# Window attention feeding a rational-activation MLP on one core: the sink rows of V in one transfer per batch, V in two pieces per head, another program order

## The chip, the cores and the metric

The kernel runs on one NeuronCore of a Trainium2 chip. The metric is device time in microseconds (us) of one execution. TensorE (PE) does the matrix products, VectorE (DVE) and ScalarE (ACT) the elementwise work, GpSimd (POOL) issues the loads that change float32 into bfloat16, and SyncE (SP) issues plain transfers and DMA transposes. Each engine runs its own instructions strictly in the order in which the program lists them, and waits on semaphores for the others.

## The reference

Four batches, eight heads, 768 tokens, head width 64. A token attends to itself, to the 127 tokens before it, and to the first four tokens of its sequence (the sink rows). The attention output, as 3072 rows of 512, goes through a two-layer network with a rational function between its layers.

```python
scores = q @ k.T / sqrt(64)
keep = (pos_k < 4) | ((pos_q - pos_k >= 0) & (pos_q - pos_k < 128))
a = softmax(where(keep, scores, -1e9)); x = (a @ v)     # per batch and head
x = x.transpose(0, 2, 1, 3).reshape(3072, 512)
h = x @ w_in                                            # 512 -> 2048
P = a0 + a1*h + a2*h**2 + a3*h**3
Q = 1 + |b0|*|h| + |b1|*h**2
out = (P / (Q + 1e-6)) @ w_out                          # 2048 -> 512
```

## The kernel before, in words

**Steps.** The 3072 tokens are cut into 12 steps of 256; three steps make a batch. For step s, four pieces `scores(s, 0..3)` (L561, L569, and L551 for the sink keys) fill a PSUM bank with masked scores, `exps(s, i)` (L581, ACT) turns each into weights, two pieces `attend(s, G)` (L622) multiply them with V, `norm(s, G)` (L630, L631, DVE) divides by the sums, and `turn_x` with `placed_x` transposes the result into `xblk`. Then four pieces `gemm1(s, j)` (L681, 16 matmuls each) make h, `copy_in` (L688, ACT) takes it out of PSUM, DVE and ACT compute the rational function (L695 to L735, with the division done as exp of minus ln on ACT), and `gemm2(s, ...)` (L742) multiplies with w_out. Step 0 and step 11 do the rational function in four parts, the others in one.

**Order.** Every piece of work is registered by `piece(...)`, with the engine that issues it. `ORDER` is a list of 728 numbers that was worked out beforehand: it names the registered pieces one by one, and a negative number stands for that many warming matmuls on a scratch tile (`spin`, L529). The table `BANK` names the PSUM buffer of a piece and `ENGINE` whether a copy runs on DVE or ACT. So the list fixes the sequence on every engine and in every queue. Data dependences, buffers that must come free, and a limited number of DMA semaphores (a later transfer that reuses one waits until the earlier one has landed) add the waits.

**The first loads.** The first 256 keys and 384 queries of batch 0 come in float32 through the queues of SP and ACT, half of the heads each (`load_k0`, L298; `load_q0`, L308), are cast (`cast_k0`, `cast_q0`, L482 on ACT, L484 on DVE), turned on TensorE with the identity (L466) and placed. Later keys and queries come through POOL (`load_kc` L333, `load_qc` L341, from step 4 on `load_k` L350 and `load_q` L320, which SP turns by DMA transposes). V comes through POOL per head (`load_v`, L357), in batch 0 as 256 tokens and then 512, in the batches 1 to 3 as all 768 in one transfer. The weights come through POOL in four transfers each (`load_w_in` L363, `load_w_out` L369).

**The sink rows of V.** `load_v_sink(b)` (L375) loads the four first rows of V of all heads, 32 rows of 64 numbers, into `stage_s`, and it does so four times, once into each group of 32 partitions: 16 transfers of 8 KB for four batches, those of batch 0 in ACT's queue, the rest in SP's. `spread_v_sink(b)` (L379, DVE) multiplies them with an indicator into `v_sink`.

**Queues before**, read off the list. SP: `load_q0(0)`, `load_k0(0)`, 12 sink-row transfers, then transposes. ACT: `load_b`, `load_q0(1)`, 4 sink-row transfers, `load_k0(1)`, `cast_q0(0)`, `load_a`, `cast_k0(1)`, then copies and exps. TensorE: 67 warming matmuls, `turn_q0` twice, 20 warming matmuls, `turn_k0` twice, `scores(0, 1)`, and so on. `ones_v(1)` (L279), which writes the ones column of the second V buffer, is the 55th piece of DVE; four of the eight V loads of batch 1 stand behind it.

Of the kernel before, what the change touches and what calls it, by code (L numbers as in the profile page):

```python
# [60 lines left out]
def kernel(  # L61
# [65 lines left out]
    BANK = {('attend', 0, 0): 'ps_o',  # L127
             ('attend', 0, 1): 'ps_h',
             ('attend', 1, 1): 'ps_h',
             ('attend', 2, 0): 'ps_o',  # L130
             ('attend', 3, 0): 'ps_h',
             ('attend', 4, 0): 'ps_h',
             ('attend', 4, 1): 'ps_h',
             ('attend', 5, 0): 'ps_h',
             ('attend', 6, 0): 'ps_o',
             ('attend', 6, 1): 'ps_o',
             ('attend', 7, 1): 'ps_h',
             ('attend', 8, 1): 'ps_o',
             ('attend', 9, 0): 'ps_o',
             ('attend', 9, 1): 'ps_o',  # L140
             ('attend', 10, 0): 'ps_h',
             ('attend', 11, 0): 'ps_o',
             ('gemm1', 0, 0): 'ps_o',
             ('gemm1', 0, 2): 'ps_m',
             ('gemm1', 0, 3): 'ps_h',
             ('gemm1', 1, 0): 'ps_m',
             ('gemm1', 1, 1): 'ps_h',
             ('gemm1', 1, 2): 'ps_o',
             ('gemm1', 1, 3): 'ps_h',
             ('gemm1', 2, 0): 'ps_o',  # L150
             ('gemm1', 2, 1): 'ps_m',
             ('gemm1', 2, 2): 'ps_o',
             ('gemm1', 2, 3): 'ps_h',
             ('gemm1', 3, 0): 'ps_m',
             ('gemm1', 3, 1): 'ps_m',
             ('gemm1', 3, 2): 'ps_m',
             ('gemm1', 4, 0): 'ps_o',
             ('gemm1', 4, 2): 'ps_m',
             ('gemm1', 4, 3): 'ps_h',
             ('gemm1', 5, 0): 'ps_m',  # L160
             ('gemm1', 5, 3): 'ps_h',
             ('gemm1', 6, 0): 'ps_o',
             ('gemm1', 6, 2): 'ps_m',
# [12 lines left out]
             ('gemm1', 11, 1): 'ps_h',
             ('gemm1', 11, 2): 'ps_m',
             ('gemm1', 11, 3): 'ps_h',
             ('gemm2', 1, 0, 0): 'ps_o',
             ('gemm2', 2, 0, 0): 'ps_m',  # L180
             ('gemm2', 5, 0, 0): 'ps_m',
             ('gemm2', 7, 0, 0): 'ps_o',
# [5 lines left out]
             ('scores', 1, 1): 'ps_m',
             ('scores', 2, 0): 'ps_m',
             ('scores', 2, 2): 'ps_m',  # L190
             ('scores', 2, 3): 'ps_o',
             ('scores', 4, 1): 'ps_m',
# [4 lines left out]
             ('scores', 6, 1): 'ps_o',
             ('scores', 6, 2): 'ps_o',
             ('scores', 6, 3): 'ps_m',
             ('scores', 7, 0): 'ps_h',  # L200
             ('scores', 7, 3): 'ps_o',
             ('scores', 8, 2): 'ps_o',
             ('scores', 9, 2): 'ps_o',
# [1 line left out]
             ('scores', 10, 2): 'ps_m',
             ('scores', 10, 3): 'ps_h',
             ('scores', 11, 1): 'ps_m',
             ('turn_k0', 1): 'ps_h',
             ('turn_kc', 1, None): 'ps_h',
# [3 lines left out]
             ('turn_qc', 3, 0): 'ps_o',
             ('turn_x', 0, 0): 'ps_o',
             ('turn_x', 1, 0): 'ps_h',
             ('turn_x', 2, 0): 'ps_o',
# [935 lines left out]
```

## Time and profile before

| | us |
|---|---|
| three timed runs: median (lowest, highest) | 257.23 (256.55, 257.94) |
| the profiled execution's own time | 258.26 |
| its span, first to last instruction | 256.5 |
| first `exps` on ACT starts | 20.25 |
| `gemm1(0, 3)` starts | 54.12 |
| TensorE busy in the span | 230.7 |
| DVE busy, ACT busy | 211.8, 210.6 |

The profile is of one execution. Times in it count from the first instruction of the span. The page's second part cuts the span into 40 slices of 6.4 us and gives a digit of busy share per slice, the granted clock of TensorE and the rate of the DMAs. The chain of waits follows the work that ended last back to its releasers.

### The profile page before, as it was taken

To read this page: it belongs to the slowest core of one execution; us is meant where nothing else is said; L and a number is where in the kernel's file an instruction comes from. 1 tells how busy PE (TensorE), PEld (TensorE's weight loads), DVE (VectorE), ACT (ScalarE), POOL (GpSimd) and SP (SyncE) were. 2 spreads that over 40 slices of the span, in tenths; PEclk is the share of its full clock that TensorE was granted. 3 is DMA by queue.
4 is the path that set the end of the run, shared out by engine and by line. 5 is a ranking of instruction groups with operands and counts; after the bars stand their busy time and mean duration, and the time that the engine had idled before them with its cause. 6 is when DMAs were issued, how large, how long until landed. Compare 5 with 4: busy or idle time off the path is not lost.

```text
span 256.5 us, 7754 instructions
## 1 busy us (share of the span) xinstructions
PE 230.7 (90%) x3475; PEld 156.2 (61%) x3475; DVE 211.8 (83%) x243; ACT 210.6 (82%) x171; POOL 73.2 (29%) x100
## 2 busy tenths in 40 slices
PE   7548479689999987999999999999999999999993
PEld 7447257568867563764855757747875657754431
DVE  2164405999989998989977999999799999999991
ACT  2117426999999898889899999999999998998980
POOL 8964571009430721349302492000000000000000
PEclk9875957999999999999999999999999999999999
DMA  5999999249999999959999599784130303001222
GB/s 140 158 183 201 125 181 91 19 64 65 160 197 149 98 178 106 109 63 121 104 170 107 63 189 118 88 166 132 28 111 3 103 1 105 0 0 55 112 82 82
DMA packets 98753, 27.12 MB, mean 106 GB/s; under 512 B 89504, under 2 KB 95648, under 8 KB 98720
## 3 DMA queue, kind: packets, MB, share of 16 engines
q0 software_dynamic: 67920, 12.98, 85.1%
q1 hardware_dynamic: 29152, 12.69, 27.4%
q10 hardware_dynamic: 1648, 0.95, 1.4%
q8 instruction: 27, 0.44, 0.8%
q14 instruction: 6, 0.05, 0.1%
HBM read 27.40 MB, written 6.29 MB: 131 GB/s over the span
## 4 chain that ended last, share of the span: by engine, by line
PE 70%; ACT 13%; DVE 6%; DMA 6%; issue 3%; SPq 0%; ACTq 0%; DVEq 0%
PE ps_o L681 11%; PE ps_m L681 10%; PE ps_h L742 10%; PE ps_m L742 9%; PE ps_h L681 8%; PE ps_o L742 8%; DMA stage_s<-in_v_dram 3%; DMA stage_a<-in_k_dram 3%; ACT hb L688 3%; ACT den L730 3%; ACT e L581 2%; PE ps_s L561 2%; ACT lnq L725 2%; PE ps_m L622 2%; DVE x_n L631 1%
## 5 line engine op out<-in xcount | busy, mean ns | idle before, releaser
L681 PEld LDWEIGHTS <-w_in_sb 128*128 128x128 bf16 x768 | 74.8, 100 | 15.0 <-issue 1.7
L742 PEld LDWEIGHTS <-g 128*128 128x128 bf16 x384 | 35.7, 98 | 43.9 <-DVE g L735 2.5
L725 ACT ACTIVATE lnq<-den,one_eps,qsc 128x4096 f32<-128x4096 bf16 (+1 forms) x18 | 47.9, 2665 | 0.1
L730 ACT ACTIVATE den<-lnq 128x4096 bf16<-128x4096 f32 (+1 forms) x18 | 44.7, 2481 | 0.1
L357 POOL DMA_DIRECT2D v<-in_v_dram x40 | 31.7, 803 | 21.7 <-DVE den L702 18.4
L681 PE MATMUL ps_o<-xblk,w_in_sb 128*128 128x256 bf16 x304 | 37.4, 278 | 0.2 <-DMA v<-in_v_dram 0.2
L742 PE MATMUL ps_h<-w_out_sb,g 128*128 128x512 bf16 x160 | 37.1, 380 | 0.2 <-DVE g L735 0.2
L681 PE MATMUL ps_m<-xblk,w_in_sb 128*128 128x256 bf16 x272 | 34.2, 281 | 0.9 <-ACT e L581 0.9
L742 PE MATMUL ps_m<-w_out_sb,g 128*128 128x512 bf16 x128 | 30.1, 380 | 0.2 <-DVE g L735 0.2
L735 DVE TENSOR_TENSOR g<-num,den 128x4096 bf16<-128x4096 bf16 (+1 forms) x18 | 28.1, 1573 | 0.7 <-ACT den L730 0.6
L719 DVE TENSOR_TENSOR sq<-sq,hb 128x4096 bf16<-128x4096 bf16 (+1 forms) x18 | 28.3, 1574 | 0.2
L706 DVE TENSOR_TENSOR den<-den,sq 128x4096 bf16<-128x4096 bf16 (+1 forms) x18 | 28.3, 1571 | 0.2
L722 DVE TENSOR_TENSOR num<-num,sq 128x4096 bf16<-128x4096 bf16 (+1 forms) x18 | 28.2, 1572 | 0.0
L581 ACT ACTIVATE e<-ps_s 128x768 bf16<-128x768 f32 (+1 forms) x24 | 21.0, 875 | 4.5 <-PE ps_s L569 4.5
L742 PE MATMUL ps_o<-w_out_sb,g 128*128 128x512 bf16 x96 | 22.4, 379 | 1.9 <-issue 1.9
L350 POOL DMA_DIRECT2D k_bf<-in_k_dram x16 | 15.0, 942 | 31.2 <-DMA kT<-k_bf 29.0
L681 PE MATMUL ps_h<-xblk,w_in_sb 128*128 128x256 bf16 x192 | 23.0, 273 | 0.3 <-ACT hb L688 0.3
L688 ACT ACTIVATE hb<-ps_m 128x1024 bf16<-128x1024 f32 x17 | 17.4, 1023 | 6.3 <-PE ps_m L681 6.2
L688 ACT ACTIVATE hb<-ps_o 128x1024 bf16<-128x1024 f32 x19 | 19.5, 1026 | 2.6 <-PE ps_o L681 2.4
L702 DVE TENSOR_SCALAR den<-hb 128x2048 uint32<-128x2048 uint32 (+1 forms) x18 | 15.9, 882 | 6.9 <-ACT hb L688 6.9
L561 PEld LDWEIGHTS <-kT 64*64 64x64 bf16 x384 | 11.8, 112 | 14.0 <-issue 10.4
L695 ACT ACTIVATE sq<-hb 128x1024 bf16<-128x1024 bf16 (+1 forms) x15 | 20.0, 1350 | 0.0
(115 smaller groups left out, 308.9 us busy)
## 6 DMA issues: line engine op xcount, KB each, us to landing
out_dram<-o_t SPq DMA_DIRECT2D x11, 512.0 KB
v<-in_v_dram POOLq DMA_DIRECT2D x24, 96.0 KB, 7.2
w_in_sb<-in_moe_w_in_dram POOLq DMA_DIRECT2D x4, 512.0 KB, 9.1
k_bf<-in_k_dram POOLq DMA_DIRECT2D x16, 128.0 KB, 8.2
w_out_sb<-in_moe_w_out_dram POOLq DMA_DIRECT2D x4, 512.0 KB, 11.8
q_bf<-in_q_dram POOLq DMA_DIRECT2D x15, 128.0 KB, 8.4
k_raw<-in_k_dram POOLq DMA_DIRECT2D x3, 256.0 KB, 5.8
v<-in_v_dram POOLq DMA_DIRECT2D x8, 64.0 KB, 11.0
```

What stands on the lines that cost most here:

```text
L357: nc.gpsimd.dma_start(out=v_fix[b % 2][half(r), g * NHF:(g + steps) * NHF, hl, 0:D], in_=v[b, h, g * TS:(g + steps) * TS, :].rearrange("(j ...
L581: nc.scalar.activation(out=data, in_=ps[:, :, c0:512], func=AF.Exp, scale=inv_sqrt_d)
L681: nc.tensor.matmul(ps[:, n, :], lhsT=w_in_all[:, c, fc * P:(fc + 1) * P], rhs=xblk[m][:, c, :], start=(c == 0), stop=(c == NDMC - 1))
L688: nc.scalar.activation(out=hb[m][:, j * GW:(j + 1) * GW], in_=ps_h.pop((m, j)).rearrange("p n c -> p (n c)"), func=AF.Copy)
L695: nc.scalar.activation(out=sq[m][:, c], in_=hb[m][:, c], func=AF.Square)
L706: nc.vector.tensor_tensor(out=den[m][:, c], in0=den[m][:, c], in1=sq[m][:, c], op=ALU.add)
L719: nc.vector.tensor_tensor(out=sq[m][:, c], in0=sq[m][:, c], in1=hb[m][:, c], op=ALU.mult)
L722: nc.vector.tensor_tensor(out=num[m][:, c], in0=num[m][:, c], in1=sq[m][:, c], op=ALU.add)
L725: nc.scalar.activation(out=lnq_fix[:, c], in_=den[m][:, c], func=AF.Ln, scale=qsc, bias=one_eps)
L730: nc.scalar.activation(out=den[m][:, c], in_=lnq_fix[:, c], func=AF.Exp, scale=-1.0)
L735: nc.vector.tensor_tensor(out=g_of[m][:, c], in0=num[m][:, c], in1=den[m][:, c], op=ALU.mult)
L742: nc.tensor.matmul(ps_out[m][:, tt, :], lhsT=g_of[m][:, co:co + P], rhs=w_out_all[:, fc, :], start=(fc == 0), stop=(fc == NFFC - 1))
```

## The change

- `load_v_sink(b)` becomes one transfer per batch, into 32 partitions. A matmul with the constant `spread` (four 32 x 32 identities side by side) copies the 32 rows into all four groups of partitions in PSUM, once for batch 0 and once for the batches 1 to 3; `spread_v_sink` reads them there. New: a cast of the rows, the making of `spread`, two matmuls (`turn_vs`).
- V of every batch comes as 256 tokens and then 512 per head: 24 transfers of 768 tokens become 24 of 256 and 24 of 512.
- `ones_v` writes both V buffers in one piece, which stands first on DVE.
- `load_a` and `load_b` get a later place than the first loads.
- New `ORDER`, `BANK` and `ENGINE`.

```diff
+    SR = P // NPB
     ENGINE = {('cast_k0', 1): 'ACT',
+               ('cast_q0', 0): 'DVE',
                ('cast_q0', 1): 'DVE',
-               ('place_k0', 0): 'ACT',
-               ('place_k0', 1): 'DVE',
-               ('place_kc', 1, None): 'ACT',
+               ('place_k0', 1): 'ACT',
+               ('place_kc', 2, None): 'ACT',
                ('place_kc', 3, None): 'ACT',
-               ('place_qc', 1, None): 'ACT',
+               ('place_qc', 0, 0): 'ACT',
+               ('place_qc', 0, 1): 'ACT',
                ('place_qc', 2, None): 'ACT',
-               ('place_qc', 3, 0): 'ACT',
+               ('place_qc', 3, 1): 'ACT',
...
-    def ones_v(n):
-        nc.vector.memset(v_fix[n].rearrange("p j h c -> p (j h) c")[:, :, D:D + 1], 1.0)
+    def ones_v():
+        for t_ in v_fix:
+            nc.vector.memset(t_.rearrange("p j h c -> p (j h) c")[:, :, D:D + 1], 1.0)
...
-    stage_s = const_pool.tile([P, B, D], FP32, name="stage_s")
+    stage_s = const_pool.tile([SR, B, D], FP32, name="stage_s")
+    sink_rows = const_pool.tile([SR, B, D], BF16, name="sink_rows")
+    spread = const_pool.tile([SR, NPB, SR], BF16, name="spread")
...
     def load_v_sink(b):
-        for i in range(NPB):
-            (nc.sync if b else nc.scalar).dma_start(out=stage_s[i * SR:(i + 1) * SR, b, :],
-                                                    in_=v[b, :, 0:NS, :])
-
-    def spread_v_sink(b):
-        nc.vector.tensor_tensor(
-            out=v_sink[:, b, :, 0:D], in0=stage_s[:, b, :].unsqueeze(1).to_broadcast([P, H, D]),
-            in1=ind.unsqueeze(2).to_broadcast([P, H, D]), op=ALU.mult)
+        (nc.sync if b else nc.scalar).dma_start(out=stage_s[:, b, :], in_=v[b, :, 0:NS, :])
+
+    def spread_tile():
+        nc.vector.tensor_copy(out=spread, in_=ident[0:SR, 0:SR].unsqueeze(1).to_broadcast(
+            [SR, NPB, SR]))
...
+    def cast_v_sink(part):
+        bs = sink_batches(part)
+        nc.vector.tensor_copy(out=sink_rows[:, bs, :], in_=stage_s[:, bs, :])
...
+    def turn_v_sink(part, bank):
+        bs = sink_batches(part)
+        ps_v[part] = full_bank(bank)[:, 0:(bs.stop - bs.start) * D].rearrange(
+            "p (b d) -> p b d", d=D)
+        nc.tensor.matmul(ps_v[part], lhsT=spread.rearrange("p i c -> p (i c)"),
+                         rhs=sink_rows[:, bs, :], start=True, stop=True)
+
+    def spread_v_sink(part):
+        bs = sink_batches(part)
+        for b in range(bs.start, bs.stop):
+            nc.vector.tensor_tensor(
+                out=v_sink[:, b, :, 0:D],
+                in0=ps_v[part][:, b - bs.start, :].unsqueeze(1).to_broadcast([P, H, D]),
+                in1=ind.unsqueeze(2).to_broadcast([P, H, D]), op=ALU.mult)
...
-        if s == 1 or g == 0:
-            n = 2 if s == 1 else 3
-            old = [("ones_v", 1)] if b == 1 else [("attended", GPB * (b - 2) + g_)
+        if g < 2:
+            n = g + 1
+            old = [("ones_v",)] if b == 1 else [("attended", GPB * (b - 2) + g_)
                                                  for g_ in range(GPB)] if b else []
             for h in range(H):
                 piece(("load_v", s, h), "POOL", 0.75, r_ + 1.0,
...
     def v_loads(s):
         b, g = divmod(s, GPB)
-        return [("load_v", GPB * b + (1 if b == 0 and g else 0), h) for h in range(H)]
+        return [("load_v", GPB * b + min(g, 1), h) for h in range(H)]
```

**The new sequence**, read off the new list up to the point where step 0's first product is complete:

```
SP    load_vs(3) load_vs(1) load_k0(0) load_vs(2) load_q0(0), then transposes
ACT   load_q0(1) load_vs(0) load_k0(1) load_b cast_k0(1) load_a place_k0(1) place_qc(0,1) place_qc(0,0)
      exps(0,3) (0,2) babs exps(0,0) (1,0) place_kc(2) place_qc(2) exps(1,3) (1,1) (0,1) (1,2) (2,2) (2,0)
      placed_x(0,1) copy_in(0,1) (0,2) exps(2,3) place_qc(3,1) ln ln exps(2,1) copy_in(0,0) exp sqa
      place_kc(3) copy_in(0,3)
POOL  constants, then kc1, kc2, qc1, qc2, the identity and the 16 V loads of batch 0, mixed, then w_in 1, w_in 2, qc3, w_in 0, kc3, w_in 3, 2 V loads of batch 1, k and q
      of step 4, 4 V loads, w_out 3, V, V(6,3) of batch 2, V, w_out 1, w_out 0, w_out 2, ...
PE    turn_k0(1) turn_q0(1) turn_k0(0) 19 warming matmuls turn_q0(0) turn_kc(1) scores(0,3) (0,2) turn_qc(1)
      scores(0,0) (1,0) turn_vs(0) turn_kc(2) turn_vs(1) turn_qc(2) scores(1,3) (0,1) (1,1) attend(0,1)
      scores(2,0) (1,2) (2,2) attend(0,0) attend(1,1) turn_x(0,0) (0,1) attend(1,0) gemm1(0,1) (0,2)
      turn_x(1,0) scores(2,3) turn_qc(3) twice attend(2,0) scores(2,1) gemm1(0,0) turn_kc(3) attend(2,1)
      turn_x(1,1) gemm1(0,3)
```

In the list before, `gemm1(0, 3)` also stands behind the other three pieces of `gemm1(0)`, all scores of the steps 0 to 2 and the attends of the steps 0 and 1; of what differs, `scores(3, 3)` stands ahead of it there, and `attend(2, 1)` in the new list. ACT's pieces up to `copy_in(0, 3)` are in the new list the exps of the steps 0 to 2, three copies out of PSUM, two ln, one exp, one square. In the list before they are the same and one exps of step 3, one ln and one exp of step 0 more.

## Rows read from the trace of the kernel before

**Rows 1.** The page, busy time per engine, and rates per slice of 6.4 us.
```profile
PE 230.7 (90%) x3475; PEld 156.2 (61%) x3475; DVE 211.8 (83%) x243; ACT 210.6 (82%) x171; POOL 73.2 (29%) x100
...
GB/s 140 158 183 201 125 181 91 19 64 65 160 197 149 98 178 106 109 63 121 104 170 107 63 189 118 88 166 132 28 111 3 103 1 105 0 0 55 112 82 82
```

**Rows 2.** Busy time of each engine in four stretches, granted clock, DMA.
```profile
core 0: us, PE busy (x) PEld busy (x) DVE busy (x) ACT busy (x) POOL busy (x), PEclk, DMA share, GB/s
0.00:20.25 20.25, 12.16 (x127) 11.01 (x129) 6.20 (x20) 3.35 (x5) 16.76 (x35) 0.86 1.30 163
20.25:54.12 33.87, 24.44 (x626) 18.64 (x626) 18.94 (x43) 22.48 (x28) 11.20 (x15) 0.78 1.47 115
54.12:252.24 198.12, 194.11 (x2728) 126.58 (x2726) 186.02 (x180) 184.12 (x139) 45.28 (x51) 1.00 1.10 98
252.24:256.50 4.26, 0.00 (x0) 0.00 (x0) 0.69 (x1) 0.60 (x1) 0.00 (x0) 1.00 0.32 123
```

**Rows 3.** The chain that ended last: start us, length us, what.
```profile
0.80 0.46 SPq L308
...
1.85 7.32 DMA stage_s<-in_v_dram
...
9.92 7.11 DMA stage_a<-in_k_dram
17.05 0.64 ACT early L482
...
29.37 3.68 issue
...
36.20 3.57 PE ps_m L681 x16
...
54.12 1.76 PE ps_h L681 x16
```

**Rows 4.** Timeline of the first 21 us: start, length, engine, line, [idle before].
```profile
1.22 7.14 PE L529 MATMUL ps_s<-warm 128*128 128x128 bf16 x67 [1.22 <-DVE warm L859]
...
1.87 8.01 ACTq L375 DMA_DIRECT2D stage_s<-in_v_dram  x4
...
9.06 0.70 DVE L484 CAST early<-stage_b 128x768 bf16<-128x768 f32 x1 [3.67 <-DMA stage_b<-in_q_dram]
...
12.13 0.85 PE L466 MATMUL ps_m<-ident,early 128*128 128x128 bf16 x6
...
14.56 0.95 DVE L484 COPY qT<-ps_m 128x768 bf16<-128x768 bf16 x1
...
20.25 0.81 ACT L581 ACTIVATE e<-ps_o 128x768 bf16<-128x768 f32 x1 [0.85 <-PE ps_o L569]
```

**Rows 5.** The line that loads w_in, its fourth transfer alone.
```profile
L363 POOL DMA_DIRECT2D w_in_sb<-in_moe_w_in_dram x1: 752/752/752, 29.9 to 29.9; - x1
...
DMA to landing us min/median/max: 8.2/8.2/8.2
```

**Rows 6.** Who waited for whom: total us, times, longest.
```profile
POOL v L357 <- DVE den L702: 18.4, 1, 18.4
...
ACT hb L688 <- PE ps_m L681: 6.2, 6, 3.7
...
ACT e L581 <- PE ps_s L569: 4.5, 2, 4.3
```

**Rows 7.** DMA issues: count, KB each, median us to landing.
```profile
v<-in_v_dram POOLq DMA_DIRECT2D x24, 96.0 KB, 7.2
...
v<-in_v_dram POOLq DMA_DIRECT2D x8, 32.0 KB, 6.0
```

**Rows 8.** Busy time and clock in three stretches of the start.
```profile
12.00:15.00 3.00, 2.82 (x30) 2.65 (x27) 1.05 (x2) 0.00 (x0) 3.00 (x6) 0.60 1.51 183
18.00:21.00 3.00, 2.31 (x40) 1.77 (x37) 0.69 (x1) 1.35 (x3) 2.94 (x5) 0.50 1.34 198
...
36.00:39.00 3.00, 2.80 (x14) 2.00 (x14) 0.00 (x0) 0.15 (x1) 1.22 (x2) 0.50 2.31 161
```

More of the change, by code (lines that the diff above doesn't have):

```diff
@@ L126 @@
                ('placed_x', 4, 1): 'DVE'}
[L127 to L136, printed above, removed]
+    BANK = {('attend', 1, 1): 'ps_o',
+             ('attend', 3, 0): 'ps_o',
+             ('attend', 5, 1): 'ps_o',
@@ L137 @@
              ('attend', 7, 1): 'ps_h',
+             ('attend', 8, 0): 'ps_o',
              ('attend', 8, 1): 'ps_o',
              ('attend', 9, 0): 'ps_o',
[L140 to L143, printed above, removed]
+             ('attend', 10, 0): 'ps_o',
+             ('attend', 10, 1): 'ps_o',
+             ('attend', 11, 0): 'ps_h',
+             ('gemm1', 0, 1): 'ps_h',
              ('gemm1', 0, 2): 'ps_m',
-             ('gemm1', 0, 3): 'ps_h',
@@ L146 @@
[L146 to L149, printed above, removed]
+             ('gemm1', 0, 3): 'ps_m',
+             ('gemm1', 1, 1): 'ps_m',
+             ('gemm1', 1, 3): 'ps_m',
              ('gemm1', 2, 0): 'ps_o',
-             ('gemm1', 2, 1): 'ps_m',
-             ('gemm1', 2, 2): 'ps_o',
-             ('gemm1', 2, 3): 'ps_h',
+             ('gemm1', 2, 1): 'ps_h',
              ('gemm1', 3, 0): 'ps_m',
-             ('gemm1', 3, 1): 'ps_m',
+             ('gemm1', 3, 1): 'ps_h',
@@ L156 @@
              ('gemm1', 3, 2): 'ps_m',
[L157 to L163, printed above, removed]
+             ('gemm1', 4, 1): 'ps_h',
+             ('gemm1', 4, 2): 'ps_o',
+             ('gemm1', 4, 3): 'ps_m',
+             ('gemm1', 5, 1): 'ps_h',
+             ('gemm1', 5, 2): 'ps_o',
@@ L164 @@
+             ('gemm1', 5, 3): 'ps_m',
+             ('gemm1', 6, 0): 'ps_m',
+             ('gemm1', 6, 1): 'ps_m',
+             ('gemm1', 6, 2): 'ps_o',
              ('gemm1', 6, 3): 'ps_m',
@@ L176 @@
[L176 to L182, printed above, removed]
+             ('gemm2', 2, 0, 0): 'ps_o',
              ('gemm2', 8, 0, 0): 'ps_m',
              ('gemm2', 9, 0, 0): 'ps_o',
-             ('scores', 0, 0): 'ps_h',
-             ('scores', 0, 1): 'ps_o',
+             ('gemm2', 10, 0, 0): 'ps_m',
@@ L187 @@
+             ('gemm2', 11, 0, 0): 'ps_h',
+             ('scores', 0, 1): 'ps_s',
+             ('scores', 0, 2): 'ps_m',
              ('scores', 1, 0): 'ps_h',
[L188 to L192, printed above, removed]
-             ('scores', 4, 2): 'ps_m',
-             ('scores', 4, 3): 'ps_o',
-             ('scores', 5, 2): 'ps_o',
-             ('scores', 5, 3): 'ps_m',
@@ L197 @@
[L197 to L203, printed above, removed]
-             ('scores', 10, 0): 'ps_h',
[L205 to L209, printed above, removed]
@@ L210 @@
-             ('turn_q0', 0): 'ps_o',
-             ('turn_q0', 1): 'ps_m',
-             ('turn_qc', 2, None): 'ps_o',
[L213 to L216, printed above, removed]
+             ('scores', 1, 1): 'ps_o',
+             ('scores', 1, 2): 'ps_o',
+             ('scores', 1, 3): 'ps_m',
+             ('scores', 2, 0): 'ps_h',
+             ('scores', 3, 1): 'ps_o',
+             ('scores', 3, 3): 'ps_o',
@@ new lines @@
+             ('scores', 4, 2): 'ps_m',
+             ('scores', 5, 0): 'ps_o',
+             ('scores', 5, 1): 'ps_h',
+             ('scores', 5, 3): 'ps_o',
+             ('scores', 6, 2): 'ps_m',
+             ('scores', 7, 1): 'ps_m',
+             ('scores', 7, 3): 'ps_h',
+             ('scores', 8, 0): 'ps_o',
+             ('scores', 9, 0): 'ps_m',
+             ('scores', 9, 2): 'ps_h',
+             ('scores', 10, 0): 'ps_h',
+             ('scores', 10, 1): 'ps_h',
+             ('scores', 10, 3): 'ps_o',
@@ new lines @@
+             ('scores', 11, 0): 'ps_m',
+             ('scores', 11, 3): 'ps_m',
+             ('turn_k0', 1): 'ps_o',
+             ('turn_kc', 3, None): 'ps_o',
+             ('turn_q0', 1): 'ps_h',
+             ('turn_qc', 1, None): 'ps_o',
+             ('turn_qc', 2, None): 'ps_o',
+             ('turn_qc', 3, 0): 'ps_h',
+             ('turn_vs', 0): 'ps_o',
+             ('turn_vs', 1): 'ps_h',
+             ('turn_x', 0, 0): 'ps_h',
+             ('turn_x', 0, 1): 'ps_o',
+             ('turn_x', 1, 0): 'ps_o',
@@ L812 @@
         piece(("load_v", 0, h), "POOL", 0.64, -25 + 0.1 * h, lambda h=h: load_v(0, h, 1),
-              [("ones_v", 0)], kind="sw", load=0.25)
+              [("ones_v",)], kind="sw", load=0.25)
     for s in range(1, NSTEP):
@@ L849 @@
     piece(("sink_consts",), "POOL", 1.0, -24.5, sink_consts)
-    piece(("load_b",), "ACT", 0.45, -38.5, load_b, kind="hw", load=0.1)
+    first = [("load_k0", 1), ("load_q0", 1)]
+    piece(("load_b",), "ACT", 0.45, -38.5, load_b, first, kind="hw", load=0.1)
     piece(("load_a",), "ACT", 0.6, -38, lambda: nc.scalar.dma_start(
-        out=a_bc, in_=moe_a.partition_broadcast(P)), kind="hw", load=0.1)
+        out=a_bc, in_=moe_a.partition_broadcast(P)), first, kind="hw", load=0.1)
     piece(("babs",), "ACT", 0.4, -14, take_abs, [("load_b",)])
@@ L860 @@
     piece(("nil",), "DVE", 0.07, -90, lambda: nc.vector.memset(nil, 0.0))
-    for n in range(2):
-        piece(("ones_v", n), "DVE", 0.12, -30, lambda n=n: ones_v(n))
+    piece(("ones_v",), "DVE", 0.12, -30, ones_v)
     for n in range(2):
@@ L868 @@
     for b in range(B):
-        piece(("load_vs", b), "SP" if b else "ACT", 1.8, -38.6 if b == 0 else -20 + b,
-              lambda b=b: load_v_sink(b), kind="hw", load=0.3)
-        piece(("spread_vs", b), "DVE", 0.6, -18 + 4 * b, lambda b=b: spread_v_sink(b),
-              [("sink_consts",), ("load_vs", b)])
+        piece(("load_vs", b), "SP" if b else "ACT", 0.5, -37.5 if b == 0 else -20 + b,
+              lambda b=b: load_v_sink(b), kind="hw", load=0.1)
+    piece(("spread",), "DVE", 0.1, -30, spread_tile, [("ident",)])
+    for part in range(2):
+        piece(("cast_vs", part), "DVE", 0.15, -24, lambda part=part: cast_v_sink(part),
+              [("load_vs", b) for b in (range(1, B) if part else (0,))])
+        home = bank_of(("turn_vs", part), "ps_m")
+        piece(("turn_vs", part), "PE", 0.1, -23,
+              lambda part=part, home=home: turn_v_sink(part, home),
+              [("cast_vs", part), ("spread",)], takes=home)
+        piece(("spread_vs", part), "DVE", 0.6, -18 + 4 * part,
+              lambda part=part: spread_v_sink(part), [("sink_consts",), ("turn_vs", part)],
+              frees=home)
     piece(("ones_vs",), "DVE", 0.12, -18.1, ones_v_sink, [("sink_consts",)])
@@ L987 @@
                   + (v_loads(s - 1) if g == 1 and G == 0 else [])
-                  + [("spread_vs", b), ("ones_vs",)]
+                  + [("spread_vs", 1 if b else 0), ("ones_vs",)]
                   + [x_ for x_ in v_loads(s) if s or x_[2] // 2 % 2 == G]
```

17 lines of the change are left out of this document (11 added, 6 removed), and 77 rows, old and new, of the table ORDER.

## The prediction

> **What bounds the kernel now.** I read the page's busy times first, then the busy time by stretch, then the chain of waits, then the timeline of the first microseconds. TensorE is busy 90% of the span and DVE and ACT over 80% [rows 1]. By stretches the average comes apart [rows 2]: from 54.12 us, where `gemm1(0, 3)` starts, to the last matmul at 252.24 TensorE is busy 194.11 of 198.12 us at the full level of its clock (2.4 GHz), so 4.0 us are idle; 4.26 us of copy and store follow. From 0 to 20.25, up to the first exps, the engines mostly wait. From 20.25 to 54.12 TensorE works 24.44 of 33.87 us at a mean granted clock of 0.78, and ACT works 22.48 and idles 11.4. So the body is bound by TensorE, with DVE (186.02) and ACT (184.12) close behind, and the start by something else; a change of order can win little in the body and much in the start.
>
> The chain names it [rows 3]: a sink-row transfer of V holds the chain from 1.85 to past 9, then the second half of K from 9.92 to 17.03, and only then come cast, turn, scores and the first exps at 20.25. The timeline shows why K is late [rows 4]: its issue stands in ACT's queue behind four sink-row transfers that take from 1.87 to 9.88 to issue. What was asked for first, 2 x 384 KB of Q and 256 KB of K, had landed at 9.06, when the cast that waited for it starts.
>
> **The change, part by part.** I price it up to one checkpoint, the start of `gemm1(0, 3)`. In both lists the same scores and gemm1 pieces stand before it on TensorE but for one piece of scores or attend, so all that follows is the same work, and a shift of the checkpoint is a shift of the end.
>
> *Sink rows and the first loads.* 16 transfers become 4, and both halves of K are asked for in the first microseconds, with ACT's `load_b` and `load_a` behind them. Now 1.28 MB of Q and K run together where 1.02 MB did. From the first issue at 0.80 to 9.06 are 8.3 us [rows 3, 4]; in proportion 10.4, so the last half lands at 11.2. In the trace K's late half needs 3.2 us from its cast at 17.05 to the first exps at 20.25 [rows 3, 4]. The half that comes last is now one of Q, half again as many columns: its cast (0.70), turn (0.85) and placement (0.95) [rows 4] sum to 2.5, against an estimated two thirds of that for K, so I take 4.0. First exps at 15.2, 5.0 earlier. Bounds: 13.0, if the halves land at 9.0 as the first three did, and 20.25, if nothing comes earlier because POOL's own loads share the same engines (rate 140 to 201 GB/s in the first slices, so already well used [rows 1]).
>
> *New work for the sinks.* One cast, one small copy, two matmuls, and `spread_v_sink` reading PSUM. A DVE pass over 512 to 768 columns takes 0.70 to 0.95 [rows 4]; three such passes are at most 2.9, and DVE had 14.9 us idle in the second stretch (18.94 of 33.87 [rows 2]). This covers them: nothing. Without cover 2.9. One wait is new: `turn_qc(2)` needs the bank of `turn_vs(0)`, which DVE frees only after the mask that follows `exps(0, 0)`; behind it on TensorE stand the scores of step 1. ACT has `exps(1, 0)` and a copy to do meanwhile, nearly 2 us by the exps of 0.81 [rows 4] and more columns. Between 0 and 2, I take 0.
>
> *Start to checkpoint.* ACT has about the same pieces to do as in the second stretch, 22.48, a few pieces less. Of its 11.4 us idle, 4.3 are one wait for scores (ps_s), which lies over the 3.68 us in which TensorE "issued" without a wait that the profile shows [rows 3, 6], and 3.7 are one wait for the first gemm1, whose 16 matmuls took 3.57 us at the low level (1.2 GHz, granted clock 0.50 in 36 to 39) against 1.76 for 16 later [rows 3, 6, 8]. 3.4 are the rest. Both large waits come from where TensorE happened to stand still, and I take neither again: 15.2 + 22.5 + 3.4 = 41.1. Upper end, with all of the idle: 49.1.
>
> *The other bound of the checkpoint.* `gemm1(0, 3)` needs the fourth w_in transfer. Before, it was issued at 29.9 and landed 8.2 later, at 38.1 [rows 5]. In both lists the same loads of K, Q, V and w_in pass through POOL's queue before it, and the rate shows transfers without a pause up to there: six slices, to 38.4, of 125 to 201 GB/s, then 91 and 19 [rows 1]. So it lands near 38.1 again, whatever the order. That is below 41.1, but it is why the start can't win more than 16 us. In the list before V of the batches stands partly behind w_in 1 and 2, now ahead; this delays `gemm1(0, 1)`, not the fourth.
>
> *V in two pieces.* 24 more issues on POOL. One issue of the kind costs 0.75 (that of w_in [rows 5]); 18 us on an engine that is busy 73.2 of 256.5 us, and 45.28 of 198.12 in the body [rows 1, 2]. The bytes are the same. Cover: the free time of POOL. Without cover, at the attend that needs the last piece, up to 8 issues, 6 us. The 18.4 us that POOL stood before `ones_v(1)` [rows 6] go, so w_out comes earlier; that costs nothing now, because gemm2 comes earlier too.
>
> Here the Trainium skill ("DMA: Bandwidth & Descriptors", section "Rules for kernel authors") speaks for one half of the change and against the other: many small transfers are to be joined into one, and below 64 KB one pays mostly overhead. The rows agree only in part: a V load of 32 KB lands 6.0 us after its issue and one of 96 KB 7.2 [rows 7], so splitting adds latency, but the transfers lie over one another. With the page's fixed cost of about 2.0 us for each of 24, one after another, the estimate would be 48 us more; by the rows none of it is on the path.
>
> *Body and tail.* 198.12 + 4.26 from the checkpoint. The new list has other banks and another interleaving; TensorE's 4.0 us of idle there could vanish or grow. I take 2 more, because the lists meet a shorter start with the same DVE and ACT load. Bounds: 4 less, and 12 more (DVE's idle in the body, 198.12 - 186.02).
>
> *Sum.* 41.1 + 198.1 + 4.3 + 2 = 245.5 as a span. The profiled execution took 258.26 with a span of 256.5, so 1.8 lie around it, and it was 1.0 above the median 257.23: 245.5 + 1.8 - 1.0 = 246.3, given as 246.
>
> **The rivals.**
>
> *The loads share (R1, 0.15).* POOL's own loads start at once and Q and K land no earlier than 15; first exps at 19, checkpoint at 45 to 47. For it: the rate of the first slices. Against: the early halves landed by 9.06 beside the same loads. Time: 251.
>
> *TensorE cold (R2, 0.10).* The 67 matmuls of the first 7 us go [rows 4]; TensorE runs the whole start at 1.2 GHz. The stretch holds 24.44 us of work at a mean clock of 0.78, about 19 at full speed, 38 at half: 14 + 38 = 52 for the checkpoint, time 255 to 257. Against: the warming did not keep the clock either, it was 0.60 in 12 to 15 and 0.50 in 18 to 21 [rows 8]. The skill's page "TensorE: Matmul & The Clock Gate" (Part 1) has it that the array is slow by default and falls back after idle time; the low rows after the idle gaps agree. By that rule the removed matmuls bought nothing lasting, and a denser start warms itself.
>
> *The body gives it back (R3, 0.10).* The saving is kept to the checkpoint, but a third of it or more is lost to banks and order, DVE being at 94% of the body: 251 to 257.
>
> *Slower (R4, 0.08).* DVE decides: TensorE reaches `gemm2(m)` of every step before the `gate` (L735) that it needs, behind which gemm1 and scores are queued. DVE in the body has 12.1 us of slack; once every one of 11 steps waits 1.3 us or more, 14 us are lost: 244.3 + 14.3 = 259. For it: DVE's load. Against: gemm2 waits for gates hardly at all in the trace, TensorE idling 4.0 us in all.
>
> **How the numbers follow.** Forecast 0.57, R1 0.15, R2 0.10, R3 0.10, R4 0.08. The forecast's own range is 241 (checkpoint at 38.1 and no added wait: 38.1 + 202.4 + 0.7) to 250. The range reaches to 255, the upper checkpoint of 49.1 with 3 us of added waits, over R1, two thirds of R3 and the cheaper part of R2; that leaves out less than 0.2. Differences within 0.5% (1.3 us) can't be told from none. Faster: forecast, R1, most of R2 and R3, 0.87. Same: 0.04, out of R2 and R3. Slower: R4 and a rest, 0.09.
>
> **What would show it.** First exps near 15 and K's second half landing before 12; the fourth w_in landing near 38; `gemm1(0, 3)` between 38 and 44; from there to the last matmul 196 to 204 us. If the exps start early and the checkpoint stays past 47, look for TensorE's clock or an "issue" gap. If the checkpoint comes by 44 and the time is above 253, the body was mis-sized. I am wrong as a whole if the first exps stay near 20.

## The result and the profile after

The changed kernel took 249.13 us (median of 4, 247.96 to 253.58) beside 257.15 for the kernel before on the same chip: a ratio of 0.9671, 95% interval 0.9602 to 0.9740. On a second chip it took 251.29 (median of 6, 249.91 to 252.72) beside 257.54, ratio 0.9778, interval 0.9725 to 0.9832. The ratio leaves out the 253.58, which lies over 1.5% above the fastest execution. So the gain is 2 to 4%, and the forecast of 246.0 was 3 us too low. The profiled execution took 247.96 with a span of 246.2, against 258.26 and 256.5: 10.3 us less.

Two lines of the page: TensorE's busy time is 11.4 us less, 7.1 of them the 67 warming matmuls [rows 4], and DVE's is what it was [rows 1]. The second line is the queue that brings instructions; it matters below.

```profile
PE 219.3 (89%) x3409; PEld 148.7 (60%) x3409; DVE 211.8 (86%) x246; ACT 209.1 (85%) x171; POOL 92.4 (38%) x124
...
q8 instruction: 26, 0.43, 0.8%
```

The four stretches of [rows 2], cut at the same events (first exps, start of `gemm1(0, 3)`, last matmul), with the same columns:

```profile
0.00:13.98 13.98, 5.03 (x71) 4.46 (x72) 4.78 (x21) 4.13 (x5) 12.28 (x29) 1.00 1.17 165
13.98:44.54 30.56, 21.60 (x650) 16.78 (x650) 17.14 (x42) 19.02 (x25) 20.62 (x30) 0.89 1.60 155
44.54:241.60 197.06, 192.63 (x2688) 127.45 (x2688) 189.14 (x184) 185.39 (x141) 59.45 (x68) 1.00 1.16 99
241.60:246.20 4.60, 0.00 (x1) 0.00 (x0) 0.69 (x1) 0.60 (x1) 0.00 (x0) 0.76 0.29 114
```

The first stretch lost 6.3 us, the second 3.3, the body 1.1, and the tail gained 0.3. Nearly all of the gain is made before the checkpoint, 54.12 before and 44.54 now.

The start, in the timeline (start, length, engine, line, [idle before]); it answers to [rows 4]. Eight transfers are issued by 3.72 and none waits; the casts of both halves of K have begun by 7.41, against 17.05 for the late half before, and the cast of the last half of Q begins at 11.17.

```profile
0.80 1.64 SPq L373 DMA_DIRECT2D stage_s<-in_v_dram  x2
0.83 0.44 ACTq L307 DMA_DIRECT2D stage_b<-in_q_dram  x1
1.31 1.26 ACTq L373 DMA_DIRECT2D stage_s<-in_v_dram  x1
2.48 0.45 SPq L297 DMA_DIRECT2D stage_a<-in_k_dram  x1
2.60 0.41 ACTq L297 DMA_DIRECT2D stage_a<-in_k_dram  x1
2.98 0.70 SPq L373 DMA_DIRECT2D stage_s<-in_v_dram  x1
3.72 0.45 SPq L307 DMA_DIRECT2D stage_b<-in_q_dram  x1
...
7.10 0.43 DVE L504 CAST early<-stage_a 128x512 bf16<-128x512 f32 x1 [3.42 <-DMA stage_a<-in_k_dram]
7.41 0.63 ACT L502 ACTIVATE early<-stage_a 128x512 bf16<-128x512 f32 x1 [5.32 <-DMA stage_a<-in_k_dram]
...
11.17 0.67 DVE L504 CAST early<-stage_b 128x768 bf16<-128x768 f32 x1
...
13.98 0.81 ACT L601 ACTIVATE e<-ps_o 128x768 bf16<-128x768 f32 x1 [0.57 <-PE ps_o L589]
```

The chain of waits between the first exps and the checkpoint still holds what I had written off [rows 3]: TensorE stands twice without a wait that the profile names ("issue"), and of the two gemm1 behind the second pause the first runs wholly at the low level of the clock and the second begins there (granted clock 0.50 from 30.33 to 35.0).

```profile
23.09 1.04 issue
...
27.67 2.66 issue
...
30.60 3.53 PE ps_h L701 x16
34.13 2.61 PE ps_m L701 x16
...
40.23 1.85 PE ps_h L701 x16
```

### The profile page after: what moved, and what is told of

Read it like the earlier page. It is cut to its first block, busy times and chain, and to the rows that moved or that the text cites. A ratio compares the mean times of both kernels' runs of the same rounds, so it can differ in the third digit from the quotient of the medians.

```text
span 246.2 us, 7625 instructions
## 1 busy us (share of the span) xinstructions
PE 219.3 (89%) x3409; PEld 148.7 (60%) x3409; DVE 211.8 (86%) x246; ACT 209.1 (85%) x171; POOL 92.4 (38%) x124
## 4 chain that ended last, share of the span: by engine, by line
DVE 43%; PE 22%; ACT 20%; issue 7%; DMA 4%; SPq 3%; DVEq 0%
DVE g L755 7%; DVE num L742 6%; PE ps_h L762 6%; DVE den L726 6%; DVE sq L739 6%; ACT hb L708 5%; ACT e L601 5%; PE ps_m L701 4%; ACT den L750 4%; PE ps_h L701 4%; DVE sq L735 4%; ACT lnq L745 4%; DVE x_n L651 3%; DVE den L722 3%; DVE num L731 3%
## 5 line engine op out<-in xcount | busy, mean ns | idle before, releaser
L762 PE MATMUL ps_h<-w_out_sb,g 128*128 128x512 bf16 x256 | 58.9, 379 | 0.8 <-DVE g L755 0.6
L356 POOL DMA_DIRECT2D v<-in_v_dram x64 | 46.4, 739 | 16.1 <-DMA w_out_sb<-in_moe_w_out_dram 8.6
L701 PE MATMUL ps_h<-xblk,w_in_sb 128*128 128x256 bf16 x256 | 32.3, 282 | 0.0
L701 PE MATMUL ps_o<-xblk,w_in_sb 128*128 128x256 bf16 x224 | 26.8, 273 | 0.3 <-ACT hb L708 0.3
L319 POOL DMA_DIRECT2D q_bf<-in_q_dram x15 | 14.9, 996 | 25.3 <-DMA qT<-q_bf 21.3
L708 ACT ACTIVATE hb<-ps_h 128x1024 bf16<-128x1024 f32 x16 | 16.6, 1040 | 7.4 <-PE ps_h L701 7.3
L349 POOL DMA_DIRECT2D k_bf<-in_k_dram x16 | 17.7, 1105 | 11.2 <-DMA kT<-k_bf 8.8
L708 ACT ACTIVATE hb<-ps_m 128x1024 bf16<-128x1024 f32 x18 | 18.8, 1045 | 2.2 <-PE ps_m L701 2.1
L642 PEld LDWEIGHTS <-e 64*64 64x64 bf16 x1216 | 13.4, 107 | 10.0 <-issue 9.7
L731 DVE TENSOR_SCALAR num<-sq,acoef 128x4096 bf16<-128x4096 bf16 (+1 forms) x18 | 18.1, 1017 | 0.0
```

The lines of the kernel that those rows point to most:

```text
L356: nc.gpsimd.dma_start(out=v_fix[b % 2][half(r), g * NHF:(g + steps) * NHF, hl, 0:D], in_=v[b, h, g * TS:(g + steps) * TS, :].rearrange("(j ...
L701: nc.tensor.matmul(ps[:, n, :], lhsT=w_in_all[:, c, fc * P:(fc + 1) * P], rhs=xblk[m][:, c, :], start=(c == 0), stop=(c == NDMC - 1))
L708: nc.scalar.activation(out=hb[m][:, j * GW:(j + 1) * GW], in_=ps_h.pop((m, j)).rearrange("p n c -> p (n c)"), func=AF.Copy)
L731: nc.vector.tensor_scalar(out=num[m][:, c], in0=sq[m][:, c], scalar1=a2, scalar2=a0, op0=ALU.mult, op1=ALU.add)
L762: nc.tensor.matmul(ps_out[m][:, tt, :], lhsT=g_of[m][:, co:co + P], rhs=w_out_all[:, fc, :], start=(fc == 0), stop=(fc == NFFC - 1))
```

## The experiments

Theory A: the gain is the first K and Q, which the sixteen sink transfers held up. Theory B: the new order does it by itself. Theory F, formed from the trace after, is about the "issue" pauses: TensorE takes its instructions in blocks, and the next block is late. A run on another chip than its neighbour is compared by its ratio to the kernel before beside it.

**Four sink transfers in the old order.**

```diff
-        for i in range(NPB):
-            (nc.sync if b else nc.scalar).dma_start(out=stage_s[i * SR:(i + 1) * SR, b, :],
-                                                    in_=v[b, :, 0:NS, :])
+        (nc.sync if b else nc.scalar).dma_start(out=stage_s[0:SR, b, :], in_=v[b, :, 0:NS, :])
```

> The kernel before, its program order untouched, with one sink transfer per batch (the first 16 partitions of stage_s) in place of four; the other three 16-partition groups of the sink rows are left zero, so 12 of the 16 transfers and their values are left out. Theory A (the gain is the K half that was issued only when the sink transfers had landed): K is issued within 3 us and lands near 7.5, the first exponentials start near 14 to 16 instead of 20.25, and the time is 251 to 253 us, 4 to 6 below the kernel before. Theory B (the gain is the new program order and its banks): K may land earlier but the order of the rest gives it back; 256 to 257.5 us.

Measured 253.46, ratio 0.9846 (0.9781 to 0.9910): 4.0 us of 258.08. In its timeline ACT issues K at 6.37 instead of 9.92:

```profile
6.37 0.38 ACTq L298 DMA_DIRECT2D stage_a<-in_k_dram  x1
...
12.24 0.63 ACT L482 ACTIVATE early<-stage_a 128x512 bf16<-128x512 f32 x1 [4.60 <-DMA stage_a<-in_k_dram]
...
15.67 0.81 ACT L581 ACTIVATE e<-ps_o 128x768 bf16<-128x768 f32 x1 [0.57 <-PE ps_o L569]
```

First exps at 15.67, 4.6 earlier than before; `gemm1(0, 3)` at 50.16, 4.0 earlier; and by the ratio 4.0 reach the end. (Each of the four groups has 32 partitions, not the 16 of the expectation.) So A holds for half of the change's gain by the first ratio of the kernel after, and for two thirds by the one of the same chip (1.5% of 3.3%, or of 2.2%). K was not issued "within 3 us": it was ninth, and the ninth transfer of SP and ACT waits.

**Sixteen sink transfers in the new order.**

```diff
-        (nc.sync if b else nc.scalar).dma_start(out=stage_s[:, b, :], in_=v[b, :, 0:NS, :])
+        for i in range(NPB):
+            (nc.sync if b else nc.scalar).dma_start(out=stage_s[i * SR:(i + 1) * SR, b, :],
+                                                    in_=v[b, :, 0:NS, :])
...
-        elif work[names[n]].run:
+        elif work[names[n]].run and names[n][0] not in ("cast_vs", "turn_vs", "spread"):
```

> The kernel after, its program order kept, with the 16 sink transfers of before (four per batch, straight to 64 partitions) and without the cast, the TensorE spread and its two matmuls. Theory A: the first K half again waits for sink transfers on its queue, the first exponentials start 3 to 6 us later than the 13.98 of the kernel after, and the time is 252 to 255 us. Theory B: 249 us within 1, as after.

Measured 265.50 (258.13 to 269.08), ratio 1.0324 (1.0205 to 1.0444): outside both forecasts. B falls, for even the fastest of the four runs, 258.13, has nothing of the gain. The other three took 264 to 269 and have no trace, so what they lost more isn't known, and that the new order with the old transfers is slower than the kernel before is not shown. In the trace, which is of the fastest, the first exps start at 22.77, 8.8 later than in the kernel after. K is issued at 6.62 and 8.39 and the last half of Q at 12.15, so DVE casts it at 20.10:

```profile
0.81 5.94 SPq L374 DMA_DIRECT2D stage_s<-in_v_dram  x8
...
6.62 0.46 ACTq L297 DMA_DIRECT2D stage_a<-in_k_dram  x1
8.39 0.42 SPq L297 DMA_DIRECT2D stage_a<-in_k_dram  x1
...
12.15 0.45 SPq L307 DMA_DIRECT2D stage_b<-in_q_dram  x1
...
20.10 0.69 DVE L506 CAST early<-stage_b 128x768 bf16<-128x768 f32 x1 [2.38 <-DMA stage_b<-in_q_dram]
```

**K first in the old order.** `load_k0(1)` goes ahead of `load_vs(0)` in ACT's queue:

```diff
+    order.remove(names.index(("load_k0", 1)))
+    order.insert(order.index(names.index(("load_vs", 0))), names.index(("load_k0", 1)))
```

> The kernel before with one step moved: the K half on ACT's queue is issued ahead of batch 0's four sink transfers; all 16 sink transfers stay. Theory A in its narrow form (what matters is the place of K in the queue, not the number of sink transfers): K lands near 7.5, the first exponentials start at 15 to 16.5, time 252 to 254 us. Theory A in its wide form (sixteen transfers hold up whatever else is issued, the query halves too): another load is late in K's place, the first exponentials at 18 to 20, 255 to 257 us. Theory B: 256 to 257.5 us.

Measured 258.70, ratio 1.0056 (1.0017 to 1.0095): no gain, and none of the three forecasts, though the wide form of A has the mechanism. K is issued at 1.86, but ACT's sink transfers now wait from 2.5 to 9.3 to be issued and the last is out at 12.7, and ACT's casts stand behind them:

```profile
1.86 0.59 ACTq L298 DMA_DIRECT2D stage_a<-in_k_dram  x1
9.28 3.43 ACTq L375 DMA_DIRECT2D stage_s<-in_v_dram  x4
...
12.76 0.84 ACT L482 ACTIVATE early<-stage_b 128x768 bf16<-128x768 f32 x1 [10.67 <-DMA stage_s<-in_v_dram]
...
14.86 0.63 ACT L482 ACTIVATE early<-stage_a 128x512 bf16<-128x512 f32 x1 [1.26 <-DMA stage_s<-in_v_dram]
```

First exps at 21.13. The number of transfers has to fall; moving K among sixteen only changes what is late.

**V whole in the new order.**

```diff
+            n = n if s == 1 else 0 if g else 3
             for h in range(H):
...
-                      lambda s=s, h=h, n=n: load_v(s, h, n), old, kind="sw", load=0.3 * n)
+                      (lambda s=s, h=h, n=n: load_v(s, h, n)) if n else None, old, kind="sw", load=0.3 * n)
```

> The kernel after with V of batches 1 to 3 in one transfer of 768 tokens per head in place of 256 and 512; the program order is kept, the first part's place in it left empty. If the split is worth nothing: 249 us within 1. If it is what frees V tiles sooner (the rival): the large transfer lands later and an attend waits for it; 250.5 to 253 us.

Measured 265.13, ratio 1.0297 (1.0208 to 1.0386), outside both. The whole V stands where the order has the first third, so three times its bytes go ahead of w_out and the next K. Two lines of the DMA issues (count, KB each, median us to landing) of this run, and below them 44 to 90 us of it:

```profile
k_bf<-in_k_dram POOLq DMA_DIRECT2D x16, 128.0 KB, 9.0
w_out_sb<-in_moe_w_out_dram POOLq DMA_DIRECT2D x4, 512.0 KB, 17.6
```

```profile
44.00:90.00 46.00, 38.56 (x492) 28.25 (x491) 35.35 (x48) 36.82 (x34) 19.57 (x23) 0.90 2.32 127
```

and of the kernel after:

```profile
k_bf<-in_k_dram POOLq DMA_DIRECT2D x16, 128.0 KB, 6.5
w_out_sb<-in_moe_w_out_dram POOLq DMA_DIRECT2D x4, 512.0 KB, 10.8
```

```profile
44.00:90.00 46.00, 44.79 (x748) 32.76 (x748) 43.70 (x58) 45.08 (x41) 27.47 (x32) 1.00 2.13 133
```

TensorE gets through 492 matmuls there instead of 748. The checkpoint is at 45.13, as after; the body takes 212.8 instead of 197.1. Whole V at the place of the second part wasn't tried, so the run prices the early place of the larger transfer, not the split as such.

**V split in the old order.**

```diff
+            split = s > 1
...
+                      (lambda s=s, h=h: (load_v(s, h, 1), load_v(s + 1, h, 2))) if split else
```

> The kernel before with V of batches 1 to 3 issued as 256 and then 512 tokens per head, both at the place where it issued 768. If the split is worth nothing, as I costed it: 257 us within 1. If twice the transfers on GpSimd's queue cost time: up to 258.5. If smaller parts land soon enough to matter: 255 to 256.

Measured 257.35, ratio 1.0017 (0.9973 to 1.0061): the split by itself, both parts at the old place, is worth nothing and costs nothing. What it allows is that the second part be put off; that this is its worth in the new order is argued from the run before this one, not shown.

**67 warming matmuls in the new kernel, and none in the old.**

```diff
+    order.insert(order.index(names.index(("warm",))) + 1, -67)      # kernel after
...
+        if n in (-2, -5, -60):                                       # kernel before
+            continue
```

> The kernel after with the 67 warming matmuls that before had, ahead of everything on TensorE, where its operands are first ready; nothing is left out. Theory F (late instruction blocks): TensorE's pauses stand again after 351 and 479 matmuls counted with the spins, 67 matmuls earlier in the real work, so in other steps of it; time 249 us within 2, the sign not foretold. Rival W (a pause belongs to a step of the work): the pauses stay before the same steps, after 418 and 546 matmuls. Warming by itself (the granted clock at the first scores) should give nothing that lasts: under 0.5 us at the first exponentials.

> The kernel before without its 67 warming matmuls at the start. If they bought nothing, since TensorE waits for K and q anyway: 257 us within 1. If they warmed the clock for the first transposes and scores: 258 to 260. Theory F: the 3.68 us pause stands again after 351 matmuls, which is 67 matmuls later in the real work.

Measured 250.13, ratio 0.9730 (0.9655 to 0.9804), the first exps at 14.58; and 256.80 (254.43 to 258.79) beside 257.27 for the kernel before. Warming is worth nothing that can be told. In the new kernel the pauses did half of what F says: the second stands at the same count of matmuls, 67 earlier in the work, and the first is gone (the 351st matmul ended at 22.67, and the fetch of the next block had ended at 20.00):

```profile
0.00:24.58 24.58, 17.03 (x479) 14.54 (x479) 11.71 (x37) 13.12 (x19) 20.84 (x40) 1.00 1.25 138
24.58:27.87 3.29, 0.01 (x2) 0.01 (x2) 0.51 (x2) 0.91 (x1) 2.96 (x5) 1.00 1.24 204
```

In the old kernel without them F's pause after 351 did not come: the 351st matmul ended at 34.6, and the fetch of the next block had ended at 33.0. (A pause of 1.09 after 478 is put down to a DMA by the profile.) Its first gemm1 ran at full clock and `gemm1(0, 3)` started at 47.85, 6.3 earlier, of which the body gave back 2.9 (201.2).

**gemm1 ahead of an attend.**

```diff
+    for name in (("scores", 2, 3), ("attend", 1, 0)):
+        order.remove(names.index(name))
+        order.insert(order.index(names.index(("gemm1", 0, 1))) + 1, names.index(name))
```

> The kernel after with two steps moved: attend(1,0) and scores(2,3) come behind gemm1(0,1) instead of ahead of it; nothing is left out. Theory F (the 2.66 us in which TensorE issues nothing at 27.67, after 479 matmuls, is the next 256 of TensorE's instructions arriving late, because the short attend matmuls use up a block faster than it is fetched beside full DMA queues): the 479th matmul now comes after the 16 long matmuls of gemm1(0,1), the block has arrived by then, the pause is under 0.7 us, checkpoint gemm1(0,3) starts 2 to 4 us sooner than 44.54, and the time is 245 to 247.5 us. Rival W (the pause belongs to attend(1,0) itself or to the w_in pieces): the pause moves with attend(1,0) to behind gemm1(0,1), 248.5 to 250 us.

Measured 248.83 (246.36 to 250.66), ratio 0.9604 (0.9512 to 0.9696). The pause after 479 is gone, as F has it, but the one after 351 was 3.74 in the profiled run instead of 1.04, and with the first exps at 15.93, as Q had landed 1.8 later, `gemm1(0, 3)` started at 47.95. No gain over the kernel after is shown.

**K and Q ahead of the sink rows, and both moves.**

```diff
+    for b in (2, 1, 3):
+        behind(("load_vs", b), ("load_q0", 0))
+    behind(("load_vs", 0), ("load_k0", 1))
+    for part in (0, 1):
+        behind(("cast_vs", part), ("k_sink", 0))
...
+    for name in (("scores", 2, 3), ("attend", 1, 0)):     # both moves only
+        behind(name, ("gemm1", 0, 1))
```

> The kernel after as it is, on the chip of the two runs beside it, for a comparison on one chip. If the gain is of the kernel and not of one chip: 0.965 to 0.973 of the kernel before, 248 to 251 us.

> The kernel after with the four sink transfers behind the K and query halves on both queues (and the two casts of the sink rows later on VectorE, where nothing needs them yet); nothing is left out. Theory A (what stands ahead of K and q in the issue order sets the first exponentials): q, the last half to land, lands 1 to 2.5 us sooner than after's 10.54, the first exponentials start near 12 instead of 13.98, and 1 to 2 us of it reach the end: 247 to 248.5 us, 1 to 2 below the kernel after beside it. Rival (the transfers in flight share the same engines, so their order doesn't matter): q lands where it did; the time of after within 0.7.

> Both moves in one kernel: the sink transfers behind K and q, and attend(1,0) with scores(2,3) behind gemm1(0,1); nothing is left out. If the two are worth their parts: 2 to 4 us below the kernel after beside it, 245 to 247.5. If the pause for the instruction block after 351 matmuls grows again as it did with the one move (3.74 us against 1.05): no better than the sink transfers behind K and q alone.

Measured beside each other: after 251.29, ratio 0.9778 (0.9725 to 0.9832); K and Q first 250.07, 0.9716 (0.9667 to 0.9766); both moves 250.57, 0.9702 (0.9632 to 0.9771). The intervals overlap, so no version is shown to beat the kernel after. The last half of Q did land sooner, at 7.04 against 11.68 beside it, but ACT's half of K did not (7.58 against 7.54): it is cast at 7.60, its turn on TensorE holds what follows, DVE comes to the cast of Q at 10.71, and the first exps start at 13.70 against 14.69. That 1.0 us was lost in the pause after 351 matmuls, 4.07 here against 0.45 beside it, and `gemm1(0, 3)` starts at 46.16 against 46.13:

```profile
0.00:22.82 22.82, 11.96 (x351) 10.11 (x351) 10.86 (x35) 12.23 (x17) 21.48 (x41) 1.00 1.38 151
22.82:26.89 4.07, 0.00 (x0) 0.00 (x0) 0.00 (x0) 0.88 (x2) 2.56 (x4) 0.82 1.30 201
```

**A quarter of w_in.**

```diff
-            out=w_in_all[:, :, f0:f1],
-            in_=moe_w_in[:, f0:f1].rearrange("(c p) f -> p c f", p=P))
+            out=w_in_all[:, 0:1, f0:f1],
+            in_=moe_w_in[0:P, f0:f1].rearrange("(c p) f -> p c f", p=P))
...
-                nc.tensor.matmul(ps[:, n, :], lhsT=w_in_all[:, c, fc * P:(fc + 1) * P],
+                nc.tensor.matmul(ps[:, n, :], lhsT=w_in_all[:, 0, fc * P:(fc + 1) * P],
```

> The kernel after with a quarter of w_in loaded: only the first 128 of its rows, in the same four pieces at the same places (three quarters of its bytes are left out), and the first projection reads that quarter four times over; every engine's list of instructions stays as it is. Theory F (the instruction block is late because its fetch stands beside full DMA queues while w_in comes in): the fetches begin within 1.5 us of the block boundary before, as the one at 21.27 did, and the two pauses after 351 and 479 matmuls, 3.7 us together in the kernel after, shrink to under 1.2; the fourth w_in piece lands before 32 instead of 37.62, gemm1(0,3) starts at 39 to 42 instead of 44.54, and the time is 243.5 to 247 us. Rival (a pause comes with the run of short attend matmuls whatever the queues hold): the pauses stay at 2.5 to 4 us together and only the wait for w_in goes: gemm1(0,3) at 43 to 45, 247 to 249.5 us.

Measured 249.24, ratio 0.9673 (0.9563 to 0.9783), `gemm1(0, 3)` at 44.69: the rival. Two pauses of this run (the last column is GB/s):

```profile
23.04:24.69 1.65, 0.00 (x1) 0.00 (x0) 0.00 (x0) 0.89 (x2) 1.65 (x4) 1.00 0.71 52
...
28.23:30.89 2.66, 0.00 (x0) 0.00 (x1) 0.00 (x0) 0.02 (x1) 0.00 (x0) 0.58 1.72 166
```

and of the kernel after:

```profile
23.09:24.14 1.05, 0.01 (x2) 0.00 (x1) 0.00 (x0) 0.89 (x2) 1.05 (x2) 1.00 1.23 187
...
27.67:30.33 2.66, 0.00 (x1) 0.00 (x0) 0.00 (x0) 0.02 (x1) 0.86 (x1) 0.73 1.50 198
```

The rate is 52 and 166 instead of 187 and 198, the first pause is longer and the second is 2.66 in both. So F's cause, the full DMA queues, is wrong for the first pause; at the second, with 166, the queues were still well filled, but taking the w_in bytes away did not shorten it either. The fourth w_in piece landed at 32.8 instead of 37.6 and nothing came earlier, so w_in doesn't bound the checkpoint either.

## Why the prediction was right, and where it was not

*First exps* (forecast 15.2, measured 13.98, bounds 13.0 to 20.25). That the sink transfers held K up is the mechanism predicted, and the first experiment shows it by itself. The issue order matters through a limit: SP and ACT issue eight transfers, and the ninth waits until the first, whose semaphore it takes again, has landed. Before, the eighth was issued at 3.48 and the ninth at 6.20; after, the last half of Q at 3.72 is the eighth. The last step is not as priced. I had the landing of Q's last half (11.2) and 4.0 behind it; it landed at 10.54, but DVE cast it only at 11.17, behind the copy of K that waited for TensorE, and where it landed at 7.04 the cast was still at 10.71. So what stood between landing and exps was partly the order on DVE, and that the first exps came within 1.2 us of the forecast does not confirm this step.

*Start to checkpoint* (forecast 25.9, measured 30.6). This is the term that was mis-sized, in both of its parts. ACT's work, taken as 22.5, was 19.0: I had named the pieces that the new list leaves for later and not taken them off. ACT's idle time, taken as 3.4, was 11.5. Of the two waits in "I take neither again" the one for scores did go (no exps of the stretch waits over 0.6), but the one for gemm1 came back larger, 6.5 us for the first piece and 1.6 for the second (total, times, longest over the whole run, the columns of [rows 6]):

```profile
ACT hb L708 <- PE ps_h L701: 7.3, 2, 6.5
...
ACT hb L708 <- PE ps_m L701: 2.1, 3, 1.6
```

Behind it stand TensorE's pauses, 1.04 and 2.66, in all 3.7 in the place of 3.68, and the low level of the clock that follows: the first two gemm1 took 3.53 and 2.61, the third 1.85, so 2.4 are lost. Without these 6.1 the checkpoint would by estimate have been at 38.4; no run of the new order shows it. In the old order the run without warming matmuls lost the pause, and there the checkpoint came 6.3 earlier. I took the pause for an accident of the order; it belongs to the count. In all profiles here every pause of TensorE over 1.4 us between 20 and 50 us stands after 351, 479 or about 606 and 734 matmuls, 128 apart, whatever step is there. And each ends alike: TensorE goes on 1.4 to 1.8 us after a 16 KB packet of the instruction queue has ended, in every row of the table.

| kernel | after matmul (us) |
|---|---|
| before | 351 (3.68) |
| before, four sink transfers | 351 (1.93), 606 (3.54) |
| before, K first | 351 (4.06) |
| after | 351 (1.04), 479 (2.66) |
| after, second run | 351 (0.45), 479 (2.66) |
| after, sixteen sink transfers | 351 (2.62), 479 (2.52) |
| after, V whole | 351 (1.08), 479 (2.05), 734 (2.58) |
| after, 67 warming matmuls | 479 (3.28), 734 (1.40) |
| after, K and Q first | 351 (4.08), 479 (1.65) |
| after, gemm1 first / both moves | 351 (3.74) / 351 (3.06) |
| after, a quarter of w_in | 351 (1.65), 479 (2.66) |

Each matmul has one weight load, so a step of 128 is 256 instructions: the 6,818 of TensorE make 26.6 steps, and the trace has 26 packets of 16 KB in the instruction queue. In the kernel after one of these starts at 27.77 and ends at 28.67, and TensorE goes on at 30.33. The Trainium skill ("Runtime: NRT & Kernel Launch", section "Instruction fetch mechanics") says that instructions come in such blocks of 256 and that the fetch is mostly hidden; the size agrees, but here up to 4.1 us of it show. So that the pauses are waits for instruction blocks is shown by three things together: the count, the two runs in which the work was moved under it, and the packets.

*Checkpoint to end* (forecast 200.1 and 4.3, measured 197.1 and 4.6). The 2 us of added waits didn't come. Between `gemm1(0, 3)` and the last matmul the kernels of the new order with the split V took 195.4 to 199.1 us, the old order 197.4 to 201.2. So where they differ most is the start, and a shift of the checkpoint is a shift of the end within 3 us; V whole broke this by 16.

*The rest.* The fourth w_in was to land near 38 and landed at 37.6. The new sink work cost nothing that shows, nor did the V issues, though POOL is busy 92.4 us instead of 73.2, as priced. But I priced the V split as if it stood alone, at 0 to 6 us. By itself it is 0; the new order loses 16 us with the whole V in the place of the first part (spans 262.6 and 246.2).

*The sum.* The span was forecast at 245.5 and measured at 246.2, which is closer than its terms: 1.2 less, 4.7 more, 3.0 less and 0.3 more nearly cancel, and that is luck. The rest of the 3 us to the median is that I took 1.0 off because the profiled execution before stood above its median; after, it stood 1.2 below.

*The shares.* The old order gains 4.0 us from fewer sink transfers. The rest of the checkpoint, 50.16 to 44.54 (46.13 in the second run of after), is the new order: 1.0 to 1.7 in the first exps, 3 to 4 from there on. For these 3 to 4 the traces have a candidate: between first exps and checkpoint ACT works 22.3 to 22.9 us in every profile of the old order and 19.0 to 19.2 in every one of the new without the 67 warming matmuls, while its idle time is 11.4 before and 11.5 after. The new order puts that much of ACT's work behind the checkpoint, and the body did not grow by it (197.1 beside 198.1). Which of its moves give the gain was not taken apart.

*The rivals.* R1 is out: the halves landed by 10.54 (11.68 in the second run). R2 is out: from the first exps to the checkpoint the granted clock was 0.89 on average (0.84 in the second run, 0.94 with the 67 matmuls) against 0.78 before, and adding or removing them changed no time that can be told. R3 and R4 are out by the body.

**What stays open.** What sets the moment at which a block is asked for. From entering a block to the beginning of the next fetch it was 0.2 to 5.7 us in these stretches; where TensorE had just stood over 1 us at the block that it entered, never under 2.4. In four profiles (after, twice; V whole; a quarter of w_in) the blocks behind 351 and 479 were entered 6.20 us apart. That the low clock is caused by the pause wasn't tried apart.

## What to carry to other kernels

Count the transfers, not the bytes, that are issued ahead of the first operands: small ones use up the few that may be out at once (eight here), and an engine that waits to issue one holds its own work as well. When the profile says "issue", count the instructions up to the gap in two kernels: if the count is the same, the pause belongs to the count, and moving work changes what stands at it and not that there is one (here the pause after 479 went and the one after 351 grew). A change that is worth nothing by itself may be what the rest of the list stands on, so take it out of the changed kernel as well as putting it into the old one.
